# A transformer block on one NeuronCore: a new hand-written order of all instructions, and another set of ordering waits for GpSimd

## The chip, the core and the metric

The kernel runs on one core of one Trainium2 chip. The core has five engines, each with its own instruction queue that is worked through in order: TensorE (PE) for matmuls, with its weight loads shown as PEld, VectorE (DVE), ScalarE (ACT), GpSimd (POOL) and SyncE (SP), which here only issues DMAs. Engines wait for each other through semaphores. The metric is the device time of one execution in microseconds.

## The reference

One transformer block over 2048 tokens of 448 features, with a modulation computed from a condition vector `c`: attention with 16 heads of 28 features and a sliding window of 256 keys, and then a gated MLP that mixes along the sequence (gMLP).

```python
mod = silu(c) @ w_mod                       # six rows: sa, ca, ga, sb, cb, gb
h = layernorm(x) * (1 + ca) + sa
q, k, v = h @ wqkv                          # 16 heads of 28
p = softmax(where(0 <= i - j < 256, q k^T * 28**-0.5, -1e9))
x = x + ga * ((p v) @ wo)
h = layernorm(x) * (1 + cb) + sb
z = gelu(h @ w_in)                          # 2048 x 1792
z1, z2 = z[:, :896], layernorm(z[:, 896:])
g = w_sp @ z2 + b_sp[:, None]               # w_sp is 2048 x 2048
x = x + gb * ((z1 * g) @ w_out)
```

## The kernel before

The tokens are 16 tiles of 128; four tiles make a block `tb`. All operations are first collected, in program order, as numbered records (`Sched.add`): each has the engines on which it can run, its code on each of these, and the operations it depends on. Nothing decides the order at run time or at build time. A string, `ORDER`, written out in the file, lists all operations; each word is a number, the engine (p PE, a ACT, v DVE, g POOL, s SP), and for some the place that it takes of a shared resource (a PSUM bank, a buffer). `Sched.order` walks through the words: the order of the words of one engine is that engine's instruction queue, and the letter chooses the engine where there is a choice. A second string, `AFTER`, lists pairs of numbers `first-then`: the second operation gets an extra dependency on the first. `Sched.waits` turns dependencies into semaphore waits and drops those that are known to hold already. The times inside `Sched.order` are estimates for that walk alone: an operation's slot is fixed by the words. Some loads of the start carry a fixed landing time there (`land`).

The operations that the change and the prediction speak of:

- 0 and 1: the two halves of x's first quarter (L371), 224 KB each; 11, 14 and 15: the other three quarters (L362, 448 KB each). 11 waits for the first modulation weights; 14 and 15 wait for nothing.
- 2: the row `c` on ACT's queue (L377). 3, 4, 5: the modulation weights of the first normalisation (L367/L368), 3 (448 KB) on ACT's queue. 12, 13: the rest of `w_mod` (1344 KB and a small piece).
- 6, 7, 8: the Q and K weights (`wq_st`): 224, 448 and 112 KB. 130 to 137 copy them, padded to 32 per head, into `WQK` (L543/L544). 9, 10: V's weights. 16, 17, 26: `wo`.
- 50 to 52: `c` through PE, tanh on ACT (L479), a product on DVE (L480); 54 to 56: the modulation matmuls (L488); 57 to 110: filler matmuls before there is work (L509), of which only some stand in `ORDER`.
- 138 to 159: statistics (L552, L555, L557, L560) and normalised rows (L572 on DVE, L576 on ACT) of the first four tiles; 160 to 171: their transposes on PE (L630) and the modulated `hT` (L637/L639); 172 to 215: Q and K of the first block in two halves of 256 tokens (L679, evictions L704/L705).
- Blocks 1 to 3: normalised rows on DVE or POOL (L572/L579), transposes on PE (block 1) or as DMA transposes on SP (blocks 2 and 3), `hT` products (L620 on ACT, L622 on DVE or POOL), then Q, K (L715, L739; evictions L725 on ACT, L726 on DVE) and V (L752; evictions L756/L757).
- Attention: 39 score groups on PE (L827), each followed by two exponentials on ACT (L860, L892), a mask product on DVE or POOL (L870; L907 and L910 on DVE alone), the products with V (L936), their division on DVE, a DMA transpose, and the output product (L959). Then the second normalisation, a DMA transpose and `hT` products (L982 on ACT, L984 on DVE or POOL).
- gMLP: the two halves of `w_in` (L1015, L1061), gelu on ACT, the normalisation of z2 (L1030 on POOL, L1033, L1052 on DVE); `w_sp` comes transposed by 32 DMA transposes into `wspA` and `wspB`; 28 long products along the sequence (L1085), 16 matmuls each, an addition on DVE (L1089), a product on POOL (L1092), and the output matmuls (L1104), additions (L1115) and stores (L1120).
- 49: a small tanh on ACT (L474), first written as a table preload.

Of the kernel before, what the change touches and what calls it, by code (L numbers as in the profile page):

```python
# [1188 lines left out]
```

## Time and profile before

| | us |
|---|---|
| median of 3 runs (lowest, highest) | 268.54 (268.53, 268.73) |
| the profiled execution | 268.43 |
| its span, first to last instruction | 266.7 |
| PE busy | 260.5 |
| DVE, ACT, POOL busy | 152.6, 131.0, 134.1 |

The page of the profile gives busy times, a chain of work that ended last (followed back from the last instruction to what released each step), groups of instructions by source line, and DMA issues. A timeline lists instructions in order of time: start, length, engine, line, operation, output<-inputs, count, and in brackets the idle time before it and what ended that. PE's ends are modelled, so a PE that is shown busy can still be waiting for part of a microsecond. A time by stretches gives the same for chosen pieces of the span. Numbers after an `L` are lines of the kernel.

### The profile page before, as it was taken

The page shows a single profiled execution, that of the slowest core. Times are in us where ns is not written, and L with a number is a line of the kernel's source. Part 1 is how long each engine was busy: PE and PEld are TensorE (multiplying, and loading weights), DVE is VectorE, ACT ScalarE, POOL GpSimd, SP SyncE. Part 2 cuts the span into 40 slices and gives each one's busy share as a digit, 9 for nine tenths or more (in the row PEclk, how much of TensorE's full clock was granted, in tenths as well). Part 3 has the DMA queues.
Part 4 walks back from the last instruction along what each step waited for, and adds up shares of the span by engine and source line. Part 5 has one row for each costly group of instructions (what it writes and reads, how often), then busy time and mean ns, then how long its engine had stood idle before and what let it go on. Part 6 is the DMA issues. An engine that isn't in the chain of part 4 may idle for free.

```text
span 266.7 us, 6861 instructions
## 1 busy us (share of the span) xinstructions
PE 260.5 (98%) x2919; PEld 136.3 (51%) x2919; DVE 152.6 (57%) x358; ACT 131.0 (49%) x189; POOL 134.1 (50%) x181
## 2 busy tenths in 40 slices
PE   7999999999999999999999999999999999999996
PEld 3664565556577666454444444444444444444454
DVE  6799999999999998887263001112203242033264
ACT  3799899999999995779996400000000000000000
POOL 7657665556599866453776004215604845030430
PEclk9999999999999999999999999999999999999999
DMA  6990425971996746448999993000000000000133
GB/s 218 327 329 18 98 44 81 129 108 37 166 207 81 116 87 95 82 99 200 178 198 188 173 193 82 0 2 1 0 0 2 0 0 0 2 17 0 52 115 94
DMA packets 66281, 25.46 MB, mean 95 GB/s; under 512 B 57797, under 2 KB 65546, under 8 KB 66250
## 3 DMA queue, kind: packets, MB, share of 16 engines
q1 hardware_dynamic: 65832, 24.52, 46.2%
q8 instruction: 23, 0.38, 0.6%
q10 hardware_dynamic: 418, 0.50, 0.5%
q14 instruction: 8, 0.07, 0.1%
HBM read 9.53 MB, written 1.84 MB: 43 GB/s over the span
## 4 chain that ended last, share of the span: by engine, by line
PE 85%; ACT 7%; DMA 2%; DVE 2%; POOL 1%; SPq 1%; issue 0%
PE ps L1085 36%; PE ps L1015 8%; PE ps L1061 8%; PE ps L1104 8%; PE ps L715 5%; ACT PA L860 5%; PE ps L827 5%; PE ps L936 4%; PE ps L752 4%; PE ps L959 3%; PE ps L679 2%; ACT PA L892 2%; DMA wq_st<-in_A_wqkv_dram 2%; POOL PA L870 1%; POOL rs_all L560 1%; DVE PA L910 0%
## 5 line engine op out<-in xcount | busy, mean ns | idle before, releaser
L1092 POOL TENSOR_TENSOR z1T<-tmpg,z1T 128x512 bf16<-128x512 bf16 x28 | 31.8, 1151 | 73.8 <-DVE tmpg L1089 73.8
L1089 DVE TENSOR_TENSOR tmpg<-ps,bsp_bc 128x512 bf16<-128x512 f32 x28 | 18.8, 689 | 86.7 <-PE ps L1085 60.8
L860 ACT ACTIVATE PA<-ps 128x1536 bf16<-128x1536 f32 (+4 forms) x64 | 60.0, 974 | 1.1 <-PE ps L827 0.4
L1085 PE MATMUL ps<-wspB,z 128*128 128x512 bf16 x224 | 49.8, 379 | 0.0
L1085 PE MATMUL ps<-wspA,z 128*128 128x512 bf16 x224 | 49.3, 380 | 0.0
L1085 PEld LDWEIGHTS ps<-wspA,z 128*128 128x128 bf16 x224 | 21.8, 98 | 26.6 <-issue 0.4
L1085 PEld LDWEIGHTS ps<-wspB,z 128*128 128x128 bf16 x224 | 21.9, 98 | 26.3 <-DVE tmpg L1089 0.2
L560 POOL TENSOR_TENSOR rs_all<-ve_all,neghalf 128x1 f32<-128x1 f32 (+1 forms) x31 | 22.5, 734 | 4.5 <-DVE ve_all L557 4.0
L936 PEld LDWEIGHTS ps<-Vaug,PA 128*128 128x128 bf16 x720 | 20.9, 96 | 5.2 <-issue 1.2
L1015 PE MATMUL ps<-w_in,hT 64*128 64x448 bf16 x224 | 22.7, 350 | 0.0
L936 PE MATMUL ps<-Vaug,PA 128*128 128x32 bf16 x720 | 22.5, 177 | 0.0
L1061 PE MATMUL ps<-hT,w_in 64*128 64x512 bf16 x196 | 22.3, 376 | 0.0
L1104 PE MATMUL ps<-w_out_g,z1T 128*128 128x448 bf16 (+3 forms) x126 | 22.2, 332 | 0.0
L715 PE MATMUL ps<-hT,WQK 128*128 128x512 bf16 x80 | 20.0, 380 | 0.0
L870 POOL TENSOR_TENSOR PA<-PA,mask 128x1024 bf16<-128x1024 bf16 x7 | 15.5, 2209 | 8.5 <-ACT PA L860 3.0
L827 PE MATMUL ps<-qT,KT 32*64 32x64 bf16 (+3 forms) x768 | 18.0, 224 | 1.6 <-ACT PA L860 0.5
L552 DVE BATCH_NORM_STATS2 st_all<-x_sb 128x6 f32<-128x448 bf16 x32 | 19.2, 612 | 0.4 <-DMA x_sb<-in_A_x_dram 0.4
L892 ACT ACTIVATE PA<-ps 128x1536 bf16<-128x1536 f32 (+1 forms) x16 | 16.4, 1025 | 2.3 <-PE ps L827 2.1
L907 DVE TENSOR_TENSOR PA<-PA,mask 128x2048 bf16<-128x2048 bf16 x14 | 17.0, 1217 | 0.4 <-ACT PA L860 0.3
L1104 PEld LDWEIGHTS ps<-w_out_g,z1T 128*128 128x128 bf16 x126 | 11.7, 98 | 10.1 <-DVE fin L1115 0.2
L579 POOL TENSOR_SCALAR xn<-x_sb,rs_all,ve_all 128x448 bf16<-128x448 bf16 x18 | 14.0, 781 | 4.9 <-DVE PA L870 1.8
L1015 PEld LDWEIGHTS ps<-w_in,hT 64*128 64x128 bf16 x224 | 10.8, 94 | 10.7 <-issue 0.4
(114 smaller groups left out, 335.0 us busy)
## 6 DMA issues: line engine op xcount, KB each, us to landing
w_in<-in_B_w_in_dram SPq DMA_DIRECT2D x8, 224.0 KB, 4.0
out_dram<-fin SPq DMA_DIRECT2D x15, 112.0 KB, 1.7
x_sb<-in_A_x_dram SPq DMA_DIRECT2D x3, 448.0 KB, 4.9
wmod<-in_w_mod_dram SPq DMA_DIRECT2D x1, 1344.0 KB, 10.7
w_out_g<-in_B_w_out_dram SPq DMA_DIRECT2D x1, 784.0 KB, 5.6
bsp_bc<-in_B_b_sp_dram SPq DMA_DIRECT2D x1, 512.0 KB, 5.1
x_sb<-in_A_x_dram SPq DMA_DIRECT2D x2, 224.0 KB, 3.6
wmod<-in_w_mod_dram SPq DMA_DIRECT2D x2, 224.0 KB, 5.0
```

Source lines behind the costliest of these rows:

```text
L552: st = [dve(0.62 if True else 0, lambda e, t=t, ci=ci, s=s: e.bn_stats(st_all[:, slot, t, ci, :], s()), deps(t), prio) for ci, s in enumer ...
L560: rs = pool(0.41 + 0.155 * len(tiles), lambda e: e.tensor_tensor(rs_all[:, slot, a:b], ve_all[:, slot, a:b], neghalf[:, 0:b - a], ALU.pow) ...
L715: m = pe(4 * MMS, [lambda e, h=h, g=g, kc=kc, tb=tb: e.matmul(ps[:, h.slot[0], :], lhsT=WQK[:, kc, 4 * g:4 * g + 4, :].rearrange("p a b -> ...
L827: return [lambda e, t=t: e.matmul(to(t), lhsT=KT[32 * t:32 * t + 32, qi, key:key + kn], rhs=qT[32 * t:32 * t + 32, qi, q0:q0 + qn], start= ...
L860: return e.activation(cols(place(kb, hf) + 64 + 768 * a, [[384, 2 * (b - a)], [1, w]]), ps[:, h.slot[0]:h.slot[0] + b - a, 2 * n * w:(2 * ...
L892: return e.activation(cols(EXTRAS[ext[n].slot[0]] + 128 * a, [[128, b - a], [512, 4], [1, 128]]), ps[:, h.slot[0]:h.slot[0] + b - a, :].re ...
L936: fns.append(lambda e, hO=hO, hd=hd, bi=bi, kb=kb, nb=nb, j=j, c=(2 * t + k) * 384 + 128 * (j - kb), half=half: e.matmul(ps[:, hO.slot[0], ...
L1015: return lambda e, kc, p0, start, stop: e.matmul(ps[:, hs[t % 2].slot[hf], 0:D], lhsT=hT[p0:p0 + 64, kc, t * 128:(t + 1) * 128], rhs=w_in[ ...
L1061: return lambda e, kc, p0, start, stop: e.matmul(ps[:, hs[b // 2].slot[b % 2], :], lhsT=w_in[p0:p0 + 64, kc, ft * 128:(ft + 1) * 128], rhs ...
L1085: m = pe(16 * MMS, [lambda e, h=h, si=si, ft=ft, tb=tb: e.matmul(ps[:, h.slot[0], :], lhsT=z2[:, si, ft * 128:(ft + 1) * 128], rhs=(wspA i ...
L1092: u = pool(1.16, lambda e, ht=ht, ft=ft, tb=tb: e.tensor_tensor(z1T[tb][:, ft, :], tmpg[:, ht.slot[0], :], z1T[tb][:, ft, :], ALU.mult), [ ...
L1104: return [lambda e, ft=ft: e.matmul(ps[:, h.slot[0], c0:c1], lhsT=z1T[t // 4][:, ft, (t % 4) * 128:(t % 4 + 1) * 128], rhs=w_out_g[:, ft, ...
```

## The change

Only the two strings change. The same operations are listed in another order (one filler matmul, 71, is left out). 23 operations change between ACT and DVE (12 from ACT, 11 to it), 3 between ACT and POOL, and 65 between POOL and DVE. The score groups stand in the same order on PE, and the sum of PE's work between the first and the last of them stays. On SP, x2 (14) goes from after V's first weights to the fifth place; x3 (15) goes ahead of the rest of `w_mod`; two of the `wo` loads go behind the first store of the modulation rows; `bsp` stands ahead of eleven of the `wspB` transposes instead of one. On ACT's queue the first two DMAs change places. On POOL the two Vaug memsets (43, 44) change places. In the tail the first product that reads `wspB` goes from ninth to seventh place, and 49 goes to the end.

`AFTER` had 20 pairs and now has 16; two pairs stand in both. The targets of the new ones are: the normalised rows 236, 283, 328, 329, 330, 647, 664, 698, 766 (L579); the `hT` products 288, 810, 812; the memset 43 (twice); the weight pad 136; and the z product 975.

```diff
 ORDER = """
-2.a 27.v 38.g 0.s 36.g 28.v 29.v 30.v 31.v 57.p.0 39.g 3.a 4.s 42.g 58.p.0 5.s 59.p.0 45.g 34.v 60.p.0 33.v 6.s
-40.g 61.p.0 46.g 1.s 47.g 62.p.0 41.g 43.g 138.v 63.p.0 7.s 50.p.0 32.v 64.p.1 139.v 8.s 51.a 140.v 144.v 65.p.1
-141.g 69.p.1 52.v 145.v 54.p.0 142.g 146.v 70.p.1 143.a.0 147.g 67.p.1 55.p 11.s 148.v.1 56.p 160.p.1 111.v 136.g
-17.s 112.v 66.p.4 161.a 71.p.4 132.g 10.s 149.v 72.p.4 162.a 187.p.0.2 163.p.3 14.s 150.v 68.p.4 155.v 164.a 151.g
-177.p.1.4 9.s 172.p.5.6 152.g 131.v 156.v 165.a 130.v 173.p 13.s 157.v 133.v 178.p 158.g 153.v 135.a 179.p 35.v
-154.v.0 174.p 12.s 175.p 159.v.1 181.p 188.p 192.a 15.s 180.p 166.p.3 48.g 195.a 169.p.5 134.g 137.a 167.v 176.p
-16.s 182.p.4.7
+3.a 27.v 45.g 0.s 34.v 64.p.0 38.g 29.v 2.a 5.s 32.v 30.v 31.v 44.g 72.p.0 62.p.0 4.s 57.p.0 6.s 61.p.0 42.g
+50.p.0 14.s 69.p.1 39.g 51.a 60.p.1 46.g 138.v 40.g 1.s 58.p.1 36.g 52.v 68.p.1 33.v 139.v 7.s 41.g 144.v 59.p.0
+140.g 63.p.0 141.g 8.s 145.v 146.v 54.p.0 142.v 147.g 143.a.0 55.p 148.v.1 11.s 56.p 160.p.1 111.v 163.p.2 132.v
+10.s 66.p.3 112.v 136.g 161.v 164.a 67.p.0 9.s 149.v 177.p.0.3 162.a 47.g 65.p.4 15.s 35.v 150.v 172.p.4.5 155.v
+151.g 70.p.1 13.s 130.a 187.p.1.6 152.g 131.v 156.v 165.v 133.a 173.p 12.s 157.g 178.p 135.v 137.a 179.p 158.g
+153.v 174.p 154.v.0 181.p 188.p 159.v.1 195.a 180.p 176.p 134.v 175.p 166.p.2 43.g 269.v 193.a 169.p.3 167.a
+182.p.7.5
...
-1049.p 804.g 1050.p 848.s 1100.p.2 1054.a 1052.a 1022.a 856.s 1053.a 858.s 49.a 1094.p.3 843.s 1021.a 1051.a 851.s
-855.s 1058.p.0 846.s 826.s 847.s 1106.p.1 1097.p.4
+1050.p 1020.a 1018.p 1019.a 854.s 1073.p.0 1022.a 1052.a 1053.a 843.s 1051.a 1021.a 1054.a 844.s 1100.p.1 858.s
+848.s 857.s 1064.p.2 853.s 849.s 1061.p.3 850.s 1070.p.4 1058.p.5 1160.p.6
...
-1196.p 1193.v.3 1194.a 1197.v.0 1198.s
+1196.p 1193.v.1 1194.a 1197.v.0 1198.s 49.a
 """
-AFTER = "53-367 468-467 459-562 392-290 446-335 383-281 522-810 328-327 159-48 280-283 400-290 417-128 409-126 413-330 425-430 510-613 509-813 514-810 665-681 821-819"
+AFTER = "159-43 421-329 413-330 400-288 750-766 530-664 522-810 132-136 154-43 235-236 281-283 404-328 510-647 614-812 817-698 998-975"
```

(The two long lines of `ORDER` are broken here to be read.)

More of the change, by code (lines that the diff above doesn't have):

```diff
@@ new lines @@
+3.a 27.v 45.g 0.s 34.v 64.p.0 38.g 29.v 2.a 5.s 32.v 30.v 31.v 44.g 72.p.0 62.p.0 4.s 57.p.0 6.s 61.p.0 42.g 50.p.0 14.s 69.p.1 39.g 51.a 60.p.1 46.g 138.v 40.g 1.s 58.p.1 36.g 52.v 68.p.1 33.v 139.v 7.s 41.g 144.v 59.p.0 140.g 63.p.0 141.g 8.s 145.v 146.v 54.p.0 142.v 147.g 143.a.0 55.p 148.v.1 11.s 56.p 160.p.1 111.v 163.p.2 132.v 10.s 66.p.3 112.v 136.g 161.v 164.a 67.p.0 9.s 149.v 177.p.0.3 162.a 47.g 65.p.4 15.s 35.v 150.v 172.p.4.5 155.v 151.g 70.p.1 13.s 130.a 187.p.1.6 152.g 131.v 156.v 165.v 133.a 173.p 12.s 157.g 178.p 135.v 137.a 179.p 158.g 153.v 174.p 154.v.0 181.p 188.p 159.v.1 195.a 180.p 176.p 134.v 175.p 166.p.2 43.g 269.v 193.a 169.p.3 167.a 182.p.7.5 170.v 189.p 183.p 168.v 171.a 191.p 184.p 224.v 190.p 192.a 185.p 186.p 203.p.2 199.a 228.v 198.a 200.p.3 230.v 211.a 202.p.1 194.a 197.v 196.a 201.p.2 225.v 208.a 231.v 53.v 229.v 204.p.0 210.a 226.v 209.a 212.a 227.v 372.p.0.0 275.v 232.g 233.g 222.p.0 273.v 373.a.0 216.p.1 234.v 274.v 235.v.0 374.a 271.v 364.p.0.1 236.g.1 207.p.6 365.a.0 217.v 218.p.5 48.g 223.v 237.g.2 206.p.1 238.v.3 215.a 368.p.0.4 366.a 219.v 239.p.3 369.a 367.g 205.p.5 240.v 242.p.2 241.v 214.a 276.v 243.v 376.p.0.2 370.a 113.p.1 272.v 377.a.1 244.v 37.g 270.v 259.p.0 114.v 371.v 116.s 378.a 380.p.0.1 277.v 247.p.1 375.v 17.s 381.a 278.g 384.v 115.s 245.p.3 213.v 117.s 248.a 379.v 393.p.0.0 118.s 382.a 279.v 251.p.1 281.v.0 394.a.0 16.s 246.v 283.g.1 285.s 249.p.2 260.v 282.g.2 252.v 395.a 385.p.0.2 383.g 320.v 267.p.0 386.a.2 26.s 321.v 250.v 253.p.1 119.s 268.v 286.s 387.a 389.p.0.0 254.v 280.g.3 548.p.1 390.a 255.p.0 388.v 531.p.0 284.s 532.p 533.p 396.v 549.p 256.a 550.p 127.g 534.p 391.a 397.p.0.3 257.p.0 535.v 398.a.3 322.v 287.s 536.v.0 220.p.5 392.g 323.v 258.v 399.a 401.p.0.2 121.s 318.v 551.p 402.a 263.p.0 537.s 221.v 261.p.1 552.v 126.g 553.v.1 264.a 414.p.0.0 316.v 403.a 842.s 265.p.0 400.v 415.a.1 289.v 565.p.0 288.g 291.v 566.p 554.s 317.v 567.p 266.v 290.a 406.p.0.1 262.v 568.p 416.a 129.g 298.p.0 569.v 407.a.0 838.s 319.v 324.v 570.v.0 325.g 296.p.1 405.v 299.a 410.p.0.0 408.a 292.p.3 326.v 404.v 411.a 582.p.1 409.v 328.g.0 583.p 297.v 584.p 293.a 585.p 418.p.0.4 128.g 412.a 586.v 294.p.1 587.v.1 419.a.1 413.v 588.s 302.p.2 417.v 330.g.1 420.a 422.p.0.0 300.p.3 123.s 423.a 303.v 25.s 599.p.4 295.v 327.g.2 600.p 334.s 301.a 601.p 421.v 602.p 424.a 427.p.0.1 426.v 538.p.1 428.a.2 329.g.3 20.s 306.p.3 571.s 425.v 429.a 435.p.0.0 603.v 539.v 304.p.2 436.a.0 604.v.1 430.g 120.s 307.v 616.p.3 605.s 617.p 540.v 437.a 431.p.0.2 305.v 589.p.0 432.a 438.v 618.p 331.s 619.p 620.v 433.a 439.p.0.0 590.v 308.p.2 440.a.3 434.g 332.s 310.p.0 309.v 621.v.0 441.a 443.p.0.1 333.s 555.p.3 311.v 444.a 442.v 606.p.0 447.v 622.s 445.a 456.p.0.0 633.p.3 556.v 457.a.1 446.g 634.p 635.p 541.v 22.s 607.v 636.p 650.p.0 19.s 637.v 458.a 557.v 448.p.0.1 841.s 651.p 449.a.0 638.v.1 572.p.0 336.g 591.v 652.p 335.g 558.v 573.v 653.p 24.s 450.a 452.p.0.0 654.v 337.g 574.v 623.p.0 124.s 453.a 655.v.0 338.g 23.s 314.p.1 542.v 624.v 656.s 543.g 459.v 460.p.0.1 315.a 339.p.0 544.g 461.a.1 451.v 345.p.1 639.s 340.v 559.g 454.a 545.g.0 464.p.0.2 346.v 667.p.4 465.a 668.p 560.g 837.s 592.v 455.v 343.p.1 561.g 468.v 462.a 477.p.0.0 122.s 466.a 341.p.2 463.v 835.s 478.a.0 344.v 593.g 669.p 467.g 312.p.3 608.v 342.a 625.v 21.s 670.p 479.a 469.p.0.1 671.v 836.s 626.v 684.p.3 609.v 470.a.2 313.v 347.p.4 594.g 562.v.1 672.v.0 546.g 685.p 595.g 547.s 480.v 471.a 473.p.0.2 686.p 474.a 687.p 472.g 351.p.0 348.v 673.s 688.v 475.a 481.p.0.0 689.v.1 349.p.2 482.a.3 575.v 352.v 690.s 640.p.1 563.v 627.g 476.v 483.a 485.p.0.2 641.v 576.g 18.s 701.p.4 486.a 577.g 489.v 702.p 564.s 703.p 578.g 704.p 705.v 350.a 596.g.0 642.v 490.p.0.0 657.p.1 491.a.0 706.v.0 579.g.2 610.v 359.p.2 707.s 658.v 611.g 487.a 484.v 628.g 498.p.0.3 492.a 597.v 488.v 718.p.0 598.s 499.a.0 612.g 719.p 659.v 355.p.0 643.v 493.v 644.g 500.a 494.p.0.0 580.v 360.v 581.s 629.g 720.p 495.a 630.g.1 721.p 356.v 674.p.1 125.g 660.v 722.v 645.g 631.v 501.v 496.a 502.p.0.1 646.g 691.p.0 503.a.1 723.v.0 613.g.0 735.p.2 675.v 724.s 661.g 497.v 504.a 506.p.0.2 357.p.1 507.a 510.v 736.p 737.p 692.v 738.p 647.g.2 358.a 519.p.0.1 739.v 508.a 740.v.1 813.g 353.p.0 520.a.0 676.v 741.s 662.g 708.p.1 509.v 354.a 677.v 505.v 511.p.0.0 678.g 725.p.3 512.a.2 811.v 614.v 709.v 361.p.0 615.s 812.g 521.a 726.v 515.p.0.3 513.a 679.g 522.v 752.p.1 516.a 753.p 680.g 632.s 754.p 755.p 514.v 517.a 523.p.0.0 756.v 810.g 769.p.0 524.a.3 757.v.0 770.p 742.p.1 527.a 663.v 648.g 693.v 758.s 362.a 530.v 859.p.0 528.a 525.a 860.p.1 649.s 518.v 664.g.0 529.v 861.p 526.v 743.v 786.p.1 771.p 710.v 787.p 665.g 727.v 788.p 666.s 789.p 681.v.1 772.p 790.v 759.p.0 682.g 711.v 773.v 863.a 712.g 728.v 694.v 791.v.0 683.s 862.p 695.v 760.v 696.g 877.p.0 871.a 865.v 713.g 792.s 878.p.3 774.v.1 729.v 714.v 879.p 730.g 715.v.2 816.a 999.p.1 731.v 775.s 697.v 716.v 817.v 881.a 814.v 698.g.0 1000.p.2 761.v 872.v 717.s 762.v 880.p 882.v 815.g 763.v 1001.p 744.v 888.a 699.g 732.g.1 883.v 894.p.0 700.s 745.v 1004.a 733.v 746.g 1002.p 764.g 1003.a 747.g 793.p.0 1006.a 734.s 748.g 1005.a 776.p.1 794.v 873.a.0 749.g.2 895.p.1 777.v 765.g 896.p 778.v 750.v 897.p 795.v 751.s 898.a 766.g.0 912.p.2 796.v 779.v 906.a 780.g 900.v 913.p.0 781.g 363.s 767.v 797.v 884.v 819.a 818.v 914.p 907.g 874.v 768.s 820.v 798.g 821.v 915.p 916.a 782.g 929.p.1 875.g 783.v.1 923.a 889.v 784.v 885.g 799.v 930.p.2 785.s 886.g 890.a.0 947.p.3 924.v 800.v.2 801.v 864.v 931.p 802.s 925.a.1 917.v 948.p.0 866.v 887.v 933.a 949.p 899.v 846.s 932.p 876.v 951.a 926.v 950.p 935.v 828.s 1031.p.1 953.v 958.a 934.v 1032.p.3 901.v 941.a 936.v 918.v 845.s 902.g 927.g 1033.p 891.v 822.v 908.a.0 823.v 942.g 1034.p 824.v 839.s 919.v 825.v 1023.p.0 1037.a 867.v 909.v 805.g 1038.a 964.p.2 852.s 943.a.0 920.g 965.p.3 921.g 910.g 1036.a 966.p 827.s 1035.a 937.g 967.p 938.g 968.a 982.p.1 868.g 855.s 976.a 803.g 970.v 983.p.2 959.v 952.v 960.a.0 984.p 869.v 944.v 834.s 870.g 985.p 1024.p.3 961.v 954.v 922.v 993.a 903.g 829.s 1025.p 911.v 986.a 969.v 962.g 1039.p.2 1027.a 994.g 971.v 833.s 939.g 892.g 1040.p.1 995.a.0 893.v 1041.p 955.v 1028.a 830.s 928.v 996.g 987.v 1026.p 956.g 1044.a 972.v 1042.p 977.g 957.v 997.g 1030.a 840.s 988.v 1007.p.0 1043.a 973.g 963.v 978.a.0 28.v 989.v 1008.p.2 904.v 831.s 1029.a 1009.p 979.g 1046.a 990.g 940.g 1010.p 832.s 1011.a 1047.p.3 1045.a 945.g 1014.a 1048.p.1 851.s 905.g 1012.a 1013.a 1049.p 974.g 991.g 826.s 1015.p.0 980.g 992.v 856.s 998.v 1016.p.2 981.v 975.g 946.v 1017.p 847.s 1050.p 1020.a 1018.p 1019.a 854.s 1073.p.0 1022.a 1052.a 1053.a 843.s 1051.a 1021.a 1054.a 844.s 1100.p.1 858.s 848.s 857.s 1064.p.2 853.s 849.s 1061.p.3 850.s 1070.p.4 1058.p.5 1160.p.6 1059.v.0 1065.v.1 1066.g 809.g 1101.v.1 1154.p.2 1102.g 1060.g 1062.v.1 1063.g 1071.v.0 1067.p.1 807.g 1074.v.1 1075.g 1106.p.0 1068.v.1 1069.g 1072.g 1088.p.1 1094.p.3 1157.p.4 1166.p.5 1158.v.0 1155.v.1 1159.g 1156.g 1095.v.0 1107.v.1 1163.p.2 1108.g 1096.g 1121.p.0 1164.v.0 1161.v.1 1165.g 1162.g 1089.v.0 1090.g 1169.p.1 1172.p.2 1170.v.0 1167.v.1 1171.g 1168.g 1055.p.1 1173.v.0 1122.v.1 1123.g 808.g 1130.p.0 1056.v.1 804.g 1174.g 806.g 1057.g 1175.p.1 1176.p 1179.p.2 1183.p.3 1184.p 1079.p.4 1082.p.5 1085.p.6 1083.v.0 1127.p.5 1086.v.1 1185.v.2 1087.s 1084.s 1103.p.3 1128.v.0 1091.p.5 1180.p 1076.p.6 1181.v.0 1131.v.1 1097.p.2 1080.v.1 1132.g 1177.v.3 1081.s 1186.s 1129.g 1104.v.1 1105.g 1124.p.0 1136.p.1 1125.v.0 1092.v.1 1093.g 1139.p.0 1137.v.1 1138.g 1098.v.1 1099.g 1133.p.1 1126.g 1140.v.1 1141.g 1115.p.0 1134.v.0 1077.v.1 1135.g 1112.p.1 1078.s 1116.v.2 1182.s 1178.s 1145.p.0 1117.s 1109.p.2 1113.v.1 1114.s 1118.p.1 1110.v.0 1111.s 1151.p.2 1119.v.2 1146.v.3 1148.p.1 1147.s 1152.v.1 1120.s 1153.s 1142.p.0 1149.v.0 1150.s 1187.p.1 1143.v.3 1188.p 1191.p.2 1144.s 1189.v.2 1192.p 1195.p.0 1190.s 1196.p 1193.v.1 1194.a 1197.v.0 1198.s 49.a
```

1 line of the change is left out of this document (removed).

## The prediction

> **What bounds the kernel now.** I read the head of the page first, then the busy time by stretches, the chain of work that ended last in order of time, and last the timeline of the first microseconds, where the change moves most.
>
> ```profile
> span 266.7 us, 6861 instructions
> PE 260.5 (98%) x2919; PEld 136.3 (51%) x2919; DVE 152.6 (57%) x358; ACT 131.0 (49%) x189; POOL 134.1 (50%) x181
> PE 85%; ACT 7%; DMA 2%; DVE 2%; POOL 1%; SPq 1%; issue 0%
> ```
>
> The span is 266.7 us. The profiled execution took 268.43 us, so 1.73 us lie around the span. The median of the runs is 268.54 us, 0.11 us above this execution. The sums below start from 268.43.
>
> ```profile
> 0.00:3.00 3.00, 1.49 (x4) 0.58 (x5) 1.67 (x5) 1.18 (x1) 2.36 (x12) 1.00 0.34 85
> 3.00:6.00 3.00, 3.00 (x23) 1.06 (x22) 2.34 (x11) 0.65 (x3) 2.53 (x6) 1.00 0.97 321
> 6.00:9.00 3.00, 2.92 (x43) 1.92 (x42) 1.95 (x6) 2.08 (x4) 1.73 (x5) 1.00 1.07 336
> 10.00:100.00 90.00, 88.28 (x1779) 54.08 (x1779) 86.42 (x180) 85.56 (x109) 61.69 (x73) 1.00 0.65 123
> ```
>
> The columns are length, busy time of PE, PEld, DVE, ACT and POOL, granted clock, DMA share, GB/s. Three stages are seen. After a thin start (85 GB/s up to 3 us), from 3 to 9 us the DMA engines are full (0.97 and 1.07 of their time, 321 and 336 GB/s). From 10 to 100 us PE, DVE and ACT are all nearly full: 1.72, 3.58 and 4.44 us idle of 90. The third stage is in the chain:
>
> ```profile
> 3.51 5.51 DMA wq_st<-in_A_wqkv_dram
> 9.05 0.28 DVE WQK L543
> 9.47 1.58 PE ps L679 x13
> 15.31 0.71 PE ps L827 x64
> 146.27 72.62 PE ps L1085 x336
> ```
>
> The chain says what starts the packed part. The large QKV weight load (operation 7, issued at 3.51) lands 5.51 us later, DVE pads it, and PE runs from 9.47 on. There is little to absorb a late start behind it: the whole visible PE idle up to 100 us is 1.72 us, and from 146.27 the long product (L1085) follows on itself for 72.62 us. So I take a delay of this landing as a delay of the end.
>
> **Start: x2 is put ahead of the weights.** On SP's queue the old order issues the first x quarter's second half (1), the big weight block (7) and its tail (8), and x2 (14) only after x1 and part of wv. The new order issues 14 fifth, ahead of 1, 7 and 8. Operation 14 waits for nothing, so it is issued there at once.
>
> ```profile
> 3.04 0.43 SPq L371 DMA_DIRECT2D x_sb<-in_A_x_dram  x1
> 3.51 0.47 SPq L368 DMA_DIRECT2D wq_st<-in_A_wqkv_dram  x1
> 7.46 0.63 DVE L552 BATCH_NORM_STATS2 st_all<-x_sb 128x6 f32<-128x448 bf16 x1 [0.42 <-DMA x_sb<-in_A_x_dram]
> 9.05 0.28 DVE L543 COPY WQK<-wq_st 128x448 bf16<-128x448 bf16 x1 [0.23 <-DMA wq_st<-in_A_wqkv_dram]
> x_sb<-in_A_x_dram SPq DMA_DIRECT2D x3, 448.0 KB, 4.9
> ```
>
> The two loads issued at 3.04 and 3.51 are waited for until 7.46 and 9.05: they land in the order of issue, and late, 4.4 and 5.5 us after it. x2 is 448 KB, as large as the weight block. At 336 GB/s (448 KB are 459 kB) it takes 1.37 us; the step from 7.46 to 9.05, in which a block of that size landed, is 1.59 us. Bounds are 0 (its packets run in room that is not seen) and +1.6. I take +1.4, since DMA has no free time between 3 and 9 us. The second half of x's first quarter is late by the same, and with it its statistics and transposes, so the second QKV half gives no cover.
>
> On ACT's queue the small c row (2) now follows 448 KB of modulation weights (3), and on DVE the product that needs it (52) stands ahead of the first statistics' end (139).
>
> ```profile
> 4.43 0.25 PE L476 MATMUL ps<-one,c_row 1*128 1x1 bf16 x4
> 5.03 0.14 DVE L480 SCALAR_TENSOR_TENSOR sc_sb<-th,ps 128x4 bf16<-128x4 f32 x1
> 7.14 2.43 ACT L637 ACTIVATE hT<-ps,modT 128x256 bf16<-128x256 bf16 x4 [0.75 <-PE ps L630]
> wmod<-in_w_mod_dram ACTq DMA_DIRECT2D x1, 448.0 KB, 4.6
> ```
>
> If c lands only with the 448 KB ahead of it (issue about 0.8 and 4.6 us: 5.4), this branch moves by about 1 us, to hT products from 8.1 to 10.6; the new order shares these between ACT and DVE, so about 9.5. That is before the late weights (9.02 + 1.4 = 10.4). Cost 0 behind that cover; without it, +1.
>
> The other moves on SP have cover. x3 (15) goes ahead of the rest of wmod, and the wo loads (17, 16) go behind the first row store.
>
> ```profile
> wmod<-in_w_mod_dram SPq DMA_DIRECT2D x1, 1344.0 KB, 10.7
> 9.72 0.60 SPq L357 DMA_DIRECT2D wmod<-in_w_mod_dram  x1
> 22.44 0.94 PE L516 MATMUL ps<-wmod,sc_rep 128*32 128x448 bf16 x16
> L536 POOL TENSOR_TENSOR wo_g<-wo_g,gg_sb x4: 1035/1038/1046, 34.7 to 46.1; 128x448 bf16<-128x448 bf16 x4
> POOL hT L622 <- DVE PA L870: 5.2, 2, 3.5
> ```
>
> wmod landed near 20.4 and its reader ran at 22.44; both shift, and about 2 us cover remains. wo is read from 34.7 on; even with that issue near 26 there are over 8 us. One more transpose of x2's block now stands behind the gate load; its reader L622 waited up to 3.5 us for DVE, not for a DMA. Cost 0; the price without cover is one transpose, near 1.3 us.
>
> **Attention: the engines' shares.** The score groups (L827) keep their order on PE, and the PE work between the first and the last is the same set. Between their exponentials ACT gets 14 other operations where it had 13.
>
> ```profile
> L725 ACT ACTIVATE qT<-ps 128x512 bf16<-128x512 f32 x4 | 2.4, 600 | 0.0
> L756 ACT ACTIVATE Vaug<-ps 128x448 bf16<-128x448 f32 x6 | 3.3, 546 | 0.2 <-PE ps L752 0.2
> L704 ACT ACTIVATE qT<-ps 128x256 bf16<-128x256 f32 x7 | 2.7, 398 | 0.7 <-PE ps L679 0.6
> L982 ACT ACTIVATE hT<-hT,modT 128x512 bf16<-128x512 bf16 x4 | 3.1, 806 | 0.0
> ```
>
> Before: six V evictions at 0.55, five of 512 columns at 0.60, one at 0.40 and the gate's at 0.54, in all 7.2 us. After: five V, six of 512 columns, two at 0.40, and the hT product 290 (0.81, by L982's row), in all 8.0. So ACT has about 0.75 us more against 4.44 us idle. Bounds 0 and +0.75; I take +0.3, nearer to 0 as the idle is larger. DVE's and POOL's exchanged operations (32 from POOL to DVE, 33 back) nearly balance: with each operation at the mean of its form, DVE's sum up to its last mask differs by 0.2 us. Cost 0.
>
> The sixteen waits replace twenty; two are kept (413-330, 522-810). Nine hold a normalisation on POOL (L579), three an hT product, two the Vaug memset (43), one a weight pad (136), one a z product (975). Each holds POOL until one named DVE operation ends, at most a mask of 1.22 us; behind it queue later POOL operations, and POOL is idle 28 of 90 us. The one near an edge is 975, which must end before the long product at 146.27.
>
> ```profile
> 21.07 2.13 POOL L870 TENSOR_TENSOR PA<-PA,mask 128x1024 bf16<-128x1024 bf16 x1 [1.04 <-DVE sc_rep L483]
> L907 DVE TENSOR_TENSOR PA<-PA,mask 128x2048 bf16<-128x2048 bf16 x14 | 17.0, 1217 | 0.4 <-ACT PA L860 0.3
> L870 DVE TENSOR_TENSOR PA<-PA,mask x25: 392/681/1095, 23.3 to 101.3; 128x1024 bf16<-128x1024 bf16 x21, 128x512 bf16<-128x512 bf16 x4
> 144.18 1.09 POOL L1030 TENSOR_SCALAR z<-z,rs_all,ve_all 128x896 bf16<-128x896 bf16 x1
> ```
>
> Today it ends at 145.27, 1.0 us early, and its DVE operation (998) keeps its place; cost 0, without cover up to 0.5. A gain stands against these: the first POOL mask loses its wait of 1.04 us, in a piece where the chain went through POOL and DVE. Bounds -1.04 and 0; DVE has no less to do there, so I take -0.3.
>
> The Trainium skill ("SBUF — State Buffer", Who interferes with whom) says that a DVE operation with two SBUF inputs, issued during a GpSimd operation that reads SBUF, waits for its end. By that rule one unlucky meeting with a POOL mask costs DVE up to 2.13 us, and the sum would be 271.9. The trace here shows the worst DVE mask at 1.095 against a median of 0.681.
>
> By the rows alone a meeting costs 0.41 us. In the new order the eight masks on POOL stand among DVE operations that read PSUM or are statistics, so I take 0.
>
> **Tail.** It holds the same matmuls. The first group that reads wspB moves from ninth to seventh, and the table preload L474 goes to the end.
>
> ```profile
> 157.98 1.16 SPq L432 DMA_TRANSPOSE wspB<-in_B_w_sp_dram  x1
> wspB<-in_B_w_sp_dram SPq DMA_TRANSPOSE x16, 4.3
> 264.48 0.37 ACTq L1120 DMA_DIRECT2D out_dram<-fin  x1
> L474 ACT ACTIVATE zero<-zero 128x1 f32<-128x1 f32 x1 | 0.2, 225 | 0.0
> ```
>
> A group is 16 matmuls, 72.62/336 x 16 = 3.46 us. The seventh starts at 146.27 + 6 x 3.46 = 167.0; wspB is there by 157.98 + 4.3 = 162.3. Both shift. The preload runs beside the last output DMA (264.85 to 265.1, before 266.7). Cost 0.
>
> **Sum.** 268.43 + 1.4 (x2 ahead) + 0.3 (ACT) - 0.3 (the lost wait) = 269.8.
>
> **Rivals.** The last of them rests on two rows of the filler matmuls at the start.
>
> ```profile
> 1.51 2.98 PE L509 MATMUL ps<-tmpg 128*128 128x512 bf16 x7 [1.51 <-DVE c_row L444]
> 4.61 0.82 PE L509 MATMUL ps<-tmpg 128*128 128x512 bf16 x3
> ```
>
> - *The gaps close.* The new order takes up PE's idle of 1.72 us between 10 and 100 us. For it: three engines are nearly full and 4.44 us of ACT are free. Against: the score groups keep their order. With all of it gained and x2's landing late by only 0.4 us, 268.43 + 0.4 - 1.7 = 267.1; it decides when more than 1.4 us come back. Faster.
> - *x2 costs nothing.* DMA starts thinly (85 GB/s up to 3 us), and with wmod moved earlier on ACT's queue the room might be used. Then 268.4, no change. Against it stand the shares of 0.97 and 1.07.
> - *A second stall behind the start.* The late rows of x, one DVE meeting of 0.4 to 2.1 us and ACT's full 0.75 add to x2's 1.6: 271.2 with the small meeting.
> - *PE's clock falls back while it waits for the weights.* The first seven filler matmuls take 0.43 us each, later ones 0.22 to 0.27, though the clock column says 1.00. If 3 us of QKV after a longer wait ran at the slow pace, half of that, 1.5 us, would come on top: 271.3. PE's wait for the weights grows from some tenths to near 2 us.
>
> The Trainium skill ("TensorE: Matmul & The Clock Gate", Part 1) states that the clock halves after an idle window of about 3.4 us. By that rule a wait of 2 us keeps the clock, and the trace agrees as far as it goes, with no slow matmul after its gaps below 1 us.
>
> **How the numbers follow.** A measurement of this kernel can tell about 0.2%, 0.54 us. Chances: the forecast 0.60, gaps close 0.20, no cost 0.08, second stall 0.08, clock 0.04. Slower 0.60 + 0.08 + 0.04 with a little of the forecast's lower edge moved to the same: 0.71; same 0.09; faster 0.20. The forecast's own range is 268.9 to 270.8 (x2 1.0 to 1.6, ACT 0 to 0.75, the wait -0.5 to 0). The range for 8 in 10 reaches into both sides: 267.0 to 271.3.
>
> **What would show it.** The big weight block is waited for until about 10.4 instead of 9.05, and L679 x13 starts near 10.8 instead of 9.47; x's second half is first read near 8.8 instead of 7.46. The first score group (L827) starts near 16.7 instead of 15.31. The long product starts near 147.7 instead of 146.27 and its 117.8 us behind it stay. ACT is busy about 0.75 us more before the first gelu. If the long product starts at or before 146.3, the start's delay came back in the attention stage, and the step "little to absorb it" was wrong; if the weights land by 9.1, "in the order of issue" was.

## The result, and the profile after

| | before | after |
|---|---|---|
| median, us (lowest to highest, 6 runs each) | 268.74 (268.53 to 268.97) | 270.96 (270.26 to 271.52) |
| profiled execution, us | 268.43 | 270.55 |
| its span, us | 266.7 | 268.8 |

The changed kernel is slower: the ratio is 1.0073, 95% interval 1.0057 to 1.0090. That is 2.2 us by the medians, 2.0 us by the ratio and 2.12 us between the two profiled executions, so the two traces hold nearly all of it. The forecast was 269.8. One execution of the kernel called "after, c first" below took 1451.66 us and is left out of its ratio.

The head of the page of after:

```profile
span 268.8 us, 6839 instructions
PE 261.3 (97%) x2918; PEld 135.9 (51%) x2918; DVE 152.9 (57%) x358; ACT 130.6 (49%) x189; POOL 136.3 (51%) x181
PE 85%; ACT 8%; DVE 3%; DMA 1%; POOL 1%; issue 1%; ACTq 0%; DVEq 0%
```

The sums say little: PE is shown busy 0.8 us longer, and the other three engines by no more than 2.2 us. The busy time by stretches (length; busy time of PE, PEld, DVE, ACT, POOL; granted clock; DMA share; GB/s) says where:

```profile
3.00:6.00 3.00, 1.68 (x8) 0.46 (x7) 1.79 (x6) 0.40 (x2) 1.03 (x5) 1.00 1.05 332
6.00:9.00 3.00, 3.00 (x43) 1.73 (x42) 1.36 (x6) 0.76 (x1) 1.37 (x3) 1.00 1.08 381
10.00:100.00 90.00, 87.92 (x1765) 53.75 (x1766) 85.49 (x187) 86.06 (x110) 64.21 (x73) 1.00 0.66 122
148.30:266.00 117.70, 117.70 (x569) 55.10 (x568) 27.83 (x44) 3.04 (x6) 36.61 (x33) 1.00 0.18 40
```

From 3 to 6 us PE had been busy all 3.00 us with 23 matmuls; now it is busy 1.68 us with 8. From 10 to 100 us little changes, and the last 117.7 us are full as before. The chain of work that ended last, in order of time (start, length, what), names the cause:

```profile
1.32 3.78 DMA c_row<-in_c_dram
5.14 0.26 PE ps L476 x4
5.40 2.67 PE ps L509 x6
8.08 0.84 PE ps L488 x32
9.48 0.41 DVE hT L639
9.89 0.54 DVE st_all L552
11.39 0.90 POOL rs_all L560
13.02 0.40 DVE xn L572
17.69 0.71 PE ps L827 x64
148.41 69.17 PE ps L1085 x320
```

Before, the chain came from the QKV weights (landed at 9.02). Now it comes from the small row `c`, which arrives at 5.10, goes through six filler matmuls and the modulation product, a product hT on DVE at 9.48, and only then the statistics of x's second half, whose data had landed at 9.02, 0.8 us before DVE read them at 9.81. The first score group starts at 17.69 instead of 15.31 (+2.38), the long product at 148.41 instead of 146.27 (+2.14). So all of the loss is made ahead of the first score group.

The timeline of after at the places that the prediction named (start, length, engine, line, operation, and in brackets the idle time before it and what ended that):

```profile
0.80 0.49 ACTq L368 DMA_DIRECT2D wmod<-in_w_mod_dram  x1
1.32 0.59 ACTq L377 DMA_DIRECT2D c_row<-in_c_dram  x1
4.83 0.63 DVE L552 BATCH_NORM_STATS2 st_all<-x_sb 128x6 f32<-128x448 bf16 x1 [1.02 <-DMA x_sb<-in_A_x_dram]
5.14 0.26 PE L476 MATMUL ps<-one,c_row 1*128 1x1 bf16 x4 [1.32 <-DMA c_row<-in_c_dram]
9.81 0.62 DVE L552 BATCH_NORM_STATS2 st_all<-x_sb 128x6 f32<-128x448 bf16 x1
10.84 1.51 ACT L543 ACTIVATE WQK<-wq_st 128x448 bf16<-128x448 bf16 x3 [0.35 <-DMA wq_st<-in_A_wqkv_dram]
11.74 1.70 PE L679 MATMUL ps<-hT,WQK 128*128 128x256 bf16 x14 [0.52 <-DVE WQK L543]
```

The weights are waited for until 10.84, where 10.4 was forecast. The statistics at 9.81 wait for no data: nothing stands in brackets, DVE comes straight from the product hT.

### The profile page after: what moved, and what is told of

Read it like the earlier page. It is cut to its first block, busy times and chain, and to the rows that moved or that the text cites. A ratio compares the mean times of both kernels' runs of the same rounds, so it can differ in the third digit from the quotient of the medians.

```text
span 268.8 us, 6839 instructions
## 1 busy us (share of the span) xinstructions
PE 261.3 (97%) x2918; PEld 135.9 (51%) x2918; DVE 152.9 (57%) x358; ACT 130.6 (49%) x189; POOL 136.3 (51%) x181
## 4 chain that ended last, share of the span: by engine, by line
PE 85%; ACT 8%; DVE 3%; DMA 1%; POOL 1%; issue 1%; ACTq 0%; DVEq 0%
PE ps L1085 36%; PE ps L1104 8%; PE ps L1015 8%; PE ps L715 6%; PE ps L1061 6%; PE ps L827 5%; PE ps L936 5%; PE ps L752 4%; ACT PA L860 4%; PE ps L959 4%; ACT PA L892 2%; DMA c_row<-in_c_dram 1%; DVE st_all L552 1%; PE ps L509 1%; DVE hT L984 1%; ACT qT L704 1%
## 5 line engine op out<-in xcount | busy, mean ns | idle before, releaser
L1085 PE MATMUL ps<-wspB,z 128*128 128x512 bf16 x224 | 49.2, 379 | 0.0
L560 POOL TENSOR_TENSOR rs_all<-ve_all,neghalf 128x1 f32<-128x1 f32 (+1 forms) x31 | 21.2, 689 | 4.8 <-DVE ve_all L557 3.4
L579 POOL TENSOR_SCALAR xn<-x_sb,rs_all,ve_all 128x448 bf16<-128x448 bf16 x20 | 17.7, 886 | 10.2 <-DVE PA L907 2.9
L1115 DVE TENSOR_TENSOR fin<-ps,x_sb 128x448 bf16<-128x448 f32 (+3 forms) x18 | 10.0, 570 | 21.5 <-PE ps L1104 19.3
L870 POOL TENSOR_TENSOR PA<-PA,mask 128x1024 bf16<-128x1024 bf16 x8 | 17.4, 2173 | 6.6 <-ACT PA L860 6.6
```

Of the source, the lines that this page charges most:

```text
L560: rs = pool(0.41 + 0.155 * len(tiles), lambda e: e.tensor_tensor(rs_all[:, slot, a:b], ve_all[:, slot, a:b], neghalf[:, 0:b - a], ALU.pow) ...
L1085: m = pe(16 * MMS, [lambda e, h=h, si=si, ft=ft, tb=tb: e.matmul(ps[:, h.slot[0], :], lhsT=z2[:, si, ft * 128:(ft + 1) * 128], rhs=(wspA i ...
```

## The experiments

Two of them put one part of the change into the old order, the others take parts out of the new one. Each was timed against before on the same chip. The rows were not all measured on one chip, so two rows are compared best by their ratios. Of the edits only the words that move are shown.

| kernel | median, us | ratio to before, 95% interval |
|---|---|---|
| after | 270.96 | 1.0073 (1.0057 to 1.0090) |
| after, x2 late | 271.05 | 1.0087 (1.0074 to 1.0100) |
| after, c first | 269.81 | 1.0042 (1.0029 to 1.0056) |
| after, both | 270.00 | 1.0048 (1.0031 to 1.0066) |
| before, x2 early | 270.38 | 1.0075 (1.0049 to 1.0101) |
| before, c behind | 269.99 | 1.0043 (1.0018 to 1.0068) |
| old start, new rest | 268.99 | 1.0014 (0.9998 to 1.0030) |
| after, c first, x2 behind the QKV weights | 269.60 | 1.0028 (1.0017 to 1.0039) |
| the same and part 4 ahead of 5 | 269.03 | 1.0002 (0.9988 to 1.0016) |
| the same and hT on ACT | 268.90 | 1.0001 (0.9992 to 1.0010) |
| the same, three fillers fewer | 269.26 | 1.0016 (1.0003 to 1.0029) |
| after without six fillers | 271.29 | 1.0090 (1.0068 to 1.0113) |
| after, x2 late, without six fillers | 271.21 | 1.0093 (1.0071 to 1.0115) |

**The two suspects taken out: x2's place and c's place.** The theory of the prediction (x2 ahead of the weights) against what the trace of after shows (c).

```diff
-50.p.0 14.s 69.p.1
+50.p.0 69.p.1
...
-132.v 10.s 66.p.3
+132.v 10.s 14.s 66.p.3
```

> The new order with one word moved: x2 (14) goes back on SP behind the small V load (10), the place it has before. Theory A (x2's 448 KB ahead of the weights are what makes the start late): the weight block lands near 9.4 instead of 10.8 and the time falls by 1.2 to 1.6 us against the changed kernel, to 269.4 to 269.8. Theory B (the row c, behind 448 KB on ACT's queue, and the slow filler matmuls after it hold the start): the modulation matmuls stay where they are (near 7.9 us), and the time falls by less than 0.5 us, to 270.5 or more.

Measured: 271.05 us, nothing gained. x2's cost is not what holds the end here. The chain of this run is that of after, though its weights landed 1.1 us sooner (9.71 us against 10.82):

```profile
1.32 3.68 DMA c_row<-in_c_dram
5.31 2.67 PE ps L509 x6
9.41 0.41 DVE hT L639
```

The other suspect alone:

```diff
-3.a 27.v 45.g 0.s 34.v 64.p.0 38.g 29.v 2.a 5.s
+2.a 27.v 45.g 0.s 34.v 64.p.0 38.g 29.v 3.a 5.s
```

> The new order with the two DMAs of ACT's queue exchanged back: c (2) first, then the modulation weights (3). Theory A: c lands near 2.4 instead of 5.1, but the weight block still lands near 10.8; the time falls by less than 0.5 us, to 270.5 or more. Theory B: the modulation chain is 1 to 2 us earlier and the time falls by 1 us or more, to 269.9 or less.

Measured: 269.81 us, less than after by 1.15 us by the medians and 0.8 by the ratios. Now x's second half, which x2 delays, is what the statistics wait for (timeline of this run):

```profile
8.22 0.41 DVE L639 TENSOR_SCALAR hT<-ps,modT 128x256 bf16<-128x256 bf16 x1
9.03 0.63 DVE L552 BATCH_NORM_STATS2 st_all<-x_sb 128x6 f32<-128x448 bf16 x1 [0.40 <-DMA x_sb<-in_A_x_dram]
```

With both edits, every cost named so far should be gone:

> The new order with both put back: x2 late, c first. If A and B hold the start side by side (each covers the other): 268.2 to 268.7, more than the sum of the two single gains. If A alone: the same as with x2 late alone, within 0.3 us. If the attention stage of the new order is really 0.2 to 0.7 us shorter than before: at or below the kernel before, 268.0 to 268.6.

Measured: 270.00 us, no better than c alone; the expectation failed. The profiled execution took 270.87, the longest of the six, so its landings are on the late side. Its chain shows two new holders (three pieces of it, and x2's first reader from the timeline):

```profile
1.91 5.23 DMA wmod<-in_w_mod_dram
7.23 0.37 SPq L362
8.21 5.46 DMA x_sb<-in_A_x_dram
```

```profile
13.69 0.63 DVE L552 BATCH_NORM_STATS2 st_all<-x_sb 128x6 f32<-128x448 bf16 x1 [0.81 <-DMA x_sb<-in_A_x_dram]
14.23 0.71 DVE L639 TENSOR_SCALAR hT<-ps,modT 128x256 bf16<-128x256 bf16 x2
```

The first is part 4 of the modulation weights, which the new order issues behind part 5. It holds SP's queue too: x1 (11), which waits for these weights, is issued only at 7.23, and x2, which here stands behind it, at 8.21. The second is x2 itself: the new order puts its first statistics on DVE ahead of the products hT of the first block's second half, so x2 in its old place is now too late. The place of x2 and the order on DVE belong together.

**The same two parts put into the old order.** Do they cost there what the prediction and the first runs say?

```diff
-33.v 6.s 40.g
+33.v 6.s 14.s 40.g
...
-163.p.3 14.s 150.v
+163.p.3 150.v
```

> The kernel before with one word moved: x2 (14) goes on SP to behind the first weight load (6), as in the new order. Theory A: the weight block lands 1.2 to 1.6 us later than 9.02 and the time rises by as much, to 269.8 to 270.3. Theory B, or x2's packets finding free room: less than 0.5 us, up to 269.2.

Measured: 270.38 us, +1.66. In the trace x's second half lands 1.27 us later and the weights 1.47, and that 1.47 stands unchanged at the first score group. Chain of this run:

```profile
4.05 6.44 DMA wq_st<-in_A_wqkv_dram
10.94 1.58 PE ps L679 x13
16.78 0.70 PE ps L827 x64
```

```diff
-2.a 27.v 38.g
+3.a 27.v 38.g
...
-39.g 3.a 4.s
+39.g 2.a 4.s
```

> The order before, with one edit: on ACT's queue the c row (2) goes behind the 448 KB of modulation weights (3), as in the changed kernel; x2 stays late. Theory C (the late c holds the start by itself: c lands near 5.1 instead of 2.34, three filler matmuls of 0.43 us stand behind it, the modulation rows and with them the statistics of x's second half come about 1 us later): second half's statistics (L552) first at 8.3 to 8.8 instead of 7.46, 269.2 to 269.9 us. Theory P (the prediction's: c is hidden behind the weights, which land at 9.02): 268.5 to 268.9.

Measured: 269.99 us, +1.2, with a wide spread (268.75 to 272.76). The theory of c holds in the main (the second half's statistics start at 8.11 us, a little before the 8.3 expected, and the time is just above the range), the prediction's "hidden behind the weights" does not: the chain leaves the weights and goes through c. The profiled execution took 268.75, the shortest of the twelve, so its own delay of 0.54 us at the score group is a lower end.

```profile
1.32 3.67 DMA c_row<-in_c_dram
5.30 1.39 PE ps L509 x3
15.85 0.71 PE ps L827 x64
```

**The rest of the change.** The old order up to the first score group, then the words of the new one:

```diff
 (old words) ... 207.p.1 226.v 211.a 231.v 215.a
+269.v 53.v 229.v 204.p.0 212.a 227.v 372.p.0.0 275.v ... (new words)
...
-159-43 132-136 154-43
+159-48
```

> The order before up to the first score group (372), and from there the words of the order after (without those that already stand ahead of it), with the waits of after that belong to that part and one of before's in the start (159-48) in the place of three. Theory S (all of the loss is made ahead of the first score group, 2.38 us there, and the rest gives 0.2 back): first score group at 15.3, long product at 145.9 to 146.2, 268.2 to 268.8 us, as fast as before or a little faster. Theory R (the rest loses too, what it gives back between 20 and 31 us is only the start's delay being taken up by idle time): long product at 146.5 or later, 269.0 us or more.

Measured: 268.99 us, ratio 1.0014 (0.9998 to 1.0030), at the edge of theory R's time and above theory S's. The rest of the change is worth nothing that can be told from zero, at most a loss of 0.8 us. Timeline of this run:

```profile
15.98 0.71 PE L827 MATMUL ps<-qT,KT 32*64 32x64 bf16 x64
146.96 2.75 PE L1085 MATMUL ps<-wspA,z 128*128 128x512 bf16 x12 [0.16 <-issue]
```

The first score group is 0.67 us late, some 0.5 of it because a Q/K product (204) now stands ahead of it, which is work moved and no wait. By the score group 385, near 29 us, this run is level with before (0.06 us ahead), and at the long product, which theory R put at 146.5 or later, it is about 0.7 us behind. So in the profiled execution the rest of the new order gains a little up to 30 us and gives it back, with some more, by 146 us.

**Three edits to the DMA order.** If three late landings lie side by side, taking out one uncovers the next. This takes out all three, and leaves x2 early enough for the new order on DVE:

```diff
-3.a 27.v 45.g 0.s 34.v 64.p.0 38.g 29.v 2.a 5.s
+2.a 27.v 45.g 0.s 34.v 64.p.0 38.g 29.v 3.a 4.s
...
-62.p.0 4.s 57.p.0
+62.p.0 5.s 57.p.0
...
-50.p.0 14.s 69.p.1
+50.p.0 69.p.1
...
-141.g 8.s 145.v
+141.g 8.s 14.s 145.v
```

> The order after with three edits: c first on ACT's queue, the two parts of the modulation weights on SP back in their old places (4 ahead of 5), and x2 behind the second half of x and the QKV weights but ahead of x1 and wv. Theory T (three late landings lie side by side, each of which alone holds the statistics of x's second half to about 9 us: c, the part 4 with the modulation product on DVE, and x's own second half; taking away only one or two uncovers the next): part 4 lands near 4.7, x's second half near 7.5 to 7.9 and is read by 8.2, x2 near 11.0 to 11.6, the first score group starts by 16.1, 268.6 to 269.2 us. Rival (the new sharing of the start's work among DVE, ACT and POOL costs as much by itself): first score group later than 16.7, 269.6 us or more.

Measured: 269.03 us, ratio 1.0002: 1.9 of the 2.2 us are gone, with five words in other places (c and part 3 changed about, part 4 and part 5 changed about, x2 moved), and the rest of the new order as it is. The first score group starts at 16.33, a little later than the 16.1 expected. Up to it the chain of this run holds work of PE, DVE, POOL and ACT, and no DMA (four pieces of it):

```profile
4.02 2.67 PE ps L509 x6
8.12 0.41 DVE hT L639
8.53 0.54 DVE st_all L552
16.33 0.71 PE ps L827 x64
```

The same with part 4 left behind part 5:

> The order after with c first on ACT's queue and x2 behind the QKV weights, but part 4 of the modulation weights still behind part 5 on SP. Theory T (a part 4 that lands near 6.6 holds the modulation product, the DVE product behind it and the statistics by itself): modulation product from 6.7, statistics at 8.6 to 8.8, 269.1 to 269.5 us. Rival (the six fillers stand there till 6.7 anyway, so the swap costs nothing beside them): as with all three undone, 268.7 to 269.1 us, and then x2's place alone, behind the QKV weights and ahead of x1, made the difference to the run with x2 last.

Measured: 269.60 us, so by all executions part 4's place is worth 0.26% (1.0028 against 1.0002; the two intervals lie just apart). The trace shows that the fillers need not cover it: this time they were done early, and PE waited 0.68 us for the weights (chain of this run):

```profile
4.01 1.96 PE ps L509 x6
5.98 0.68 issue
6.65 0.17 PE ps L492
```

But the two traces do not show where 0.6 us would come from. In the run with all three edits the fillers were slow and the product started as late (6.70 in its chain); the statistics are 0.06 us apart (8.51 against 8.45), and so are the first score groups (16.39 against 16.33). That an early part 4 pays in the executions with quick fillers is likely, but not shown.

The first two products hT back from DVE to ACT, on top of the three edits:

```diff
-112.v 136.g 161.v 164.a
+112.v 136.g 161.a 164.a
...
-156.v 165.v 133.a
+156.v 165.a 133.a
```

> The order after with the three start edits (c first, part 4 ahead of part 5, x2 behind the QKV weights), all six fillers kept, and the two products hT of the first half (161, 165) on ACT as before the change. Theory D (with the late data gone, the DVE product ahead of the statistics is what is left: there it ran 8.12 to 8.53 and the statistics at 8.45 came 0.8 us after their data): statistics by 8.1, first score group by 16.0, 268.4 to 268.8 us. Rival (the product is only shifted to ACT, which is slower at it, 0.57 against 0.41 us, and delays the first QKV): first score group at 16.3 or later, 268.9 to 269.3 us.

Measured: 268.90 us, ratio 1.0001, so no difference to the run before it that can be told. The mechanism is seen, the statistics start at 7.90 instead of 8.45 and the score group at 16.08 instead of 16.33, but the end gains 0.1 us at most.

**The fillers.** Six of them ran at 0.45 us each in the chain of after. Are they a cost?

```diff
-50.p.0 14.s 69.p.1 39.g 51.a 60.p.1 46.g 138.v 40.g 1.s 58.p.1 36.g 52.v 68.p.1 33.v 139.v 7.s 41.g 144.v 59.p.0
-140.g 63.p.0 141.g
+50.p.0 14.s 39.g 51.a 46.g 138.v 40.g 1.s 36.g 52.v 33.v 139.v 7.s 41.g 144.v
+140.g 141.g
```

> The order after without the six filler matmuls (L509) between the c product (50) and the modulation product (54); nothing else. Their results are used nowhere. Theory F (c is late, and the six fillers behind it at 0.43 us each hold the modulation product 1.2 us beyond the landing of its weights, 6.6 us): the modulation product starts near 6.7 instead of 7.87, the statistics of x's second half at its landing near 9.05 instead of 9.81, 269.7 to 270.1 us. Rival (they keep PE's pace; without them the products behind run at 0.43 us a piece of 512 columns): L679 slower than before, 270.7 us or more.

Measured: 271.29 us, nothing gained, as the rival says. The hT product came 0.9 us sooner, at 8.58, but x's second half was there only at 9.59 in this execution, and so this run tells little about the fillers. The same with x2 late, so that x's second half cannot hide it:

> The order after with x2 in its old place (behind the first part of wv) and without the six filler matmuls between the c product and the modulation product; c stays behind the 448 KB. Here x's second half lands near 7.9, so it can't hide what the fillers cost. Theory F (late c plus the slow fillers behind it): modulation product from 6.7 instead of 7.78, statistics at 8.6 to 8.9 instead of 9.73, 270.0 to 270.4 us. Rival (PE without fillers runs its next products at the slow pace and gives it back, or x2 late holds a later step): 270.8 us or more.

Measured: 271.21 us (270.56 to 272.46), again nothing. Here the timeline tells why, though its execution is the longest of the six and c too came 0.9 us later than in the other runs:

```profile
6.00 0.26 PE L476 MATMUL ps<-one,c_row 1*128 1x1 bf16 x4 [2.17 <-DMA c_row<-in_c_dram]
10.11 0.63 PE L509 MATMUL ps<-tmpg 128*128 128x512 bf16 x1 [0.22 <-DVE hT L639]
12.25 2.88 PE L679 MATMUL ps<-hT,WQK 128*128 128x256 bf16 x16
```

Sixteen QKV matmuls took 2.88 us, where fourteen took 1.70 in after: without the fillers PE works at half pace until 14 us (these matmuls start 0.21 us apart up to 14.17 us, and 0.11 us apart from 14.31 on). From the first hT product to the first score group this run took 9.77 us (9.50 to 19.27), the run with x2 late and the fillers kept 8.20 (9.41 to 17.61). So in these traces the fillers cost about 1 us when c is late and spare about 1.6 us behind it. The same is seen with three of the six left out, beside the three edits and hT on ACT:

```diff
-36.g 52.v 68.p.1 33.v 139.v 7.s 41.g 144.v 59.p.0 140.g 63.p.0 141.g
+36.g 52.v 33.v 139.v 7.s 41.g 144.v 140.g 141.g
```

> The order after with the three start edits of the run before (c first on ACT's queue, part 4 of the modulation weights ahead of 5 on SP, x2 behind the QKV weights), and two more: three of the six filler matmuls between the c product and the modulation product are left out (59, 63, 68), and the two products hT of the first half (161, 165) go back from DVE to ACT. In that run the chain went through the six fillers (4.02 to 6.69) and the DVE product (8.12) to the statistics at 8.45, 0.8 us after their data landed at 7.63. Theory F (these hold what is left): modulation product from 6.3 instead of 6.49, statistics by 8.0, first score group by 15.9, 268.2 to 268.7 us. Rival (the bound is then the weight parts 3 and 5 at 6.2 and 6.7, or ACT): the same as that run, 268.8 to 269.2 us.

Measured: 269.26 us, 0.15% above the kernel with all six (1.0016 against 1.0001; the intervals overlap, so this can hardly be told). Its modulation product started at 5.06 and its statistics at 8.01, as that theory says, though the product's last part had to wait for part 5 of the weights, which landed at 6.55, as the rival says. The gain was given back at once, with the first score group at 16.76 instead of 16.08: QKV ran at half pace, and here the granted clock shows it (stretches of this run):

```profile
5.00:8.40 3.40, 2.47 (x46) 1.80 (x46) 1.90 (x9) 1.66 (x3) 1.95 (x5) 0.99 1.06 342
8.40:11.70 3.30, 3.30 (x16) 1.78 (x14) 2.54 (x11) 2.44 (x6) 1.70 (x4) 0.50 1.10 332
```

No version beats the kernel before; the best, at 268.90 us, is level with it.

## Why the prediction was right, and where not

*The sign and the place: right.* The loss comes from loads at the start, and there is little to absorb it: 2.38 us late at the first score group, 2.14 at the long product. The measured 270.96 lies in the range, but 1.16 above the number and just outside the range that was given for the forecast's own case (268.9 to 270.8). The signs that were named say the same: the weights at 10.84 (forecast 10.4), the first score group at 17.69 (16.7), the long product at 148.41 (147.7). So one term is missing.

*x2 ahead of the weights, +1.4: the size right, its part in the sum not.* Alone in the old order it costs 1.47 us in the trace and 1.66 by the medians. In the changed kernel it is covered, by 0.8 us at the statistics of x's second half: without it nothing is gained. "In the order of issue" held too, with the weights at 10.8 where 10.4 was forecast.

*The c row behind 448 KB, "cost 0 behind that cover": the step that failed.* The landing was foreseen (5.4 estimated, 5.10 measured). Its effect was followed along one branch alone, to the products hT, and compared with the weights there. Three things were left out. The words between the c product and the modulation product hold six fillers in the new order, which ran at 0.45 us each, where the old order has three at 0.27; "about 1 us" became 2.3 (the first hT product at 9.48 instead of 7.14). The product hT at 9.48 now stands on DVE ahead of the statistics of x's second half, so a late c delays the normalisation of that half, which the weights do not cover. And the first half of x landed 1.3 us later as well (first statistics at 4.83 instead of 3.59). Taking c's place back gave 1.15 us by the medians; putting it into the old order cost 1.2.

*Part 4 behind part 5: not mentioned.* The prediction went through the moves on SP and missed this swap, which the section on the change does not name either. By the medians it is worth 0.6 us once c and x2 are out of the way, though the two traces differ by only 0.06 us at the first score group; whether it costs anything while they hold the chain was not tried.

*The sum of terms.* x2 (1.66) and c (1.2) alone add up to 2.9 in the old order, and with part 4 (0.6 by the medians, in the new order) to 3.5; the whole change costs 2.2. They delay the same statistics side by side, so the latest counts and not the sum. That the forecast came near is in part luck: it left out two terms, and the one that it had was covered by one of them.

*ACT +0.3 and the lost wait -0.3.* ACT has 0.50 us more busy time from 10 to 100 us (86.06 against 85.56), of 0.75 forecast. The wait is not lost but renamed; the first POOL mask waits as long as before, now for ACT:

```profile
22.73 2.13 POOL L870 TENSOR_TENSOR PA<-PA,mask 128x1024 bf16<-128x1024 bf16 x1 [1.02 <-ACT PA L860]
```

Both terms are small. In the trace of after the lag of 2.38 us at the first score group is 1.62 at the score group 385 (31.01 against 29.39) and 2.14 at the long product: the gain is made and given back. The run with the old start bounds all of the rest together between 0 and +0.8 us.

*DVE and the sixteen waits, 0.* The longest mask on DVE is no longer than before (1.024 against 1.095 us):

```profile
L870 DVE TENSOR_TENSOR PA<-PA,mask x24: 411/680/1024, 26.1 to 102.9; 128x1024 bf16<-128x1024 bf16 x20, 128x512 bf16<-128x512 bf16 x4
```

This longest one is such a meeting, and cost 0.34 us above the median, where the prediction priced it at 0.41. It began during a normalisation on POOL (timeline of after):

```profile
91.08 0.71 POOL L579 TENSOR_SCALAR xn<-x_sb,rs_all,ve_all 128x448 bf16<-128x448 bf16 x1
91.30 1.02 DVE L870 TENSOR_TENSOR PA<-PA,mask 128x1024 bf16<-128x1024 bf16 x1
```

The operation on POOL had 0.49 us left to run. This agrees, but for some 0.15 us, with the Trainium skill's rule on such meetings ("SBUF — State Buffer", Who interferes with whom), by which the one on DVE waits for the end of the one on POOL. The 2.13 us of a meeting with a POOL mask, by which the sum would have been 271.9, did not come: in this trace no mask on DVE begins during one of POOL's eight masks. And not every meeting costs: a mask that began at 95.27, during a POOL operation on one column (L560), took 0.67 us, no more than the median.

The waits were not taken out alone, since they keep operations apart; that they cost nothing follows only for the sum of them and the rest of the order, from the run with the three edits, which keeps all sixteen and is level with before (0.9988 to 1.0016).

*The tail, 0: right.* From the first matmul of the long product to the last of PE it takes 118.1 us in both traces.

*The rivals.* "A second stall behind the start" gave the right time, 271.2, but by another mechanism (late rows of x, a DVE meeting, ACT). "PE's clock falls back" was half seen: not in QKV, which ran at full pace in after, but in the six fillers, none of which got beyond half pace (0.45 us each). PE had stood still for 1.32 us before them, but that pause is not shown to be the reason: in the run with the three edits PE went from the c product to its fillers without a pause, and its six took the same 2.67 us. "The gaps close" was seen for a stretch, 0.76 us up to 31 us, of which 0.5 was lost again by the long product.

## What to carry to other kernels

When several loads feed one early step, each of them can hold it by itself: follow every late landing to the first instruction that is queued behind its reader, also on engines that have nothing to do with it, and take the latest and not the sum. An experiment that takes out one of them and gains nothing has not shown that it is free; put the part alone into the old kernel as well. Where a small transfer shares a queue with a large one, issue the small one first: here going first gained the large one 0.1 to 0.8 us and cost the small one 2.7 to 3.1.
